# Attention into a mixture of experts on one core: later loads, split first weights, second weights behind the gathers

## The chip, the cores and the metric

The kernel runs on one core of a Trainium2 chip. The metric is the device time of one execution in microseconds. Three runs of the kernel before gave 662.02, 662.31 and 664.82 us, with a median of 662.31 us.

## The reference

Two blocks follow each other. The first is attention with 8 batches, 8 heads, 576 positions and a head size of 64. A position sees itself and the 127 before it, with a bias that falls linearly with distance by a slope of its own for each head. The second is a mixture of 8 experts over the 4608 rows of 512 that the attention gives: each row goes to the one expert with the largest gate logit.

```python
scores = scale * np.matmul(q, k.transpose(0, 1, 3, 2))
scores = np.where((rel >= 0) & (rel < 128), scores + bias[None], -1e9)
attn = softmax(scores)
x = np.matmul(attn, v)            # (8, 8, 576, 64) -> rows (4608, 512)
logits = x @ w_gate               # (4608, 8)
e = argmax(logits); g = softmax(logits)[e]
out[row] = g * (relu(x[row] @ w1[e]) @ w2[e])    # w1: 512 x 1024, w2: 1024 x 512
```

All of it is in float32.

## The kernel before

The order of the instructions on each engine is written out by hand: the program order is the order of issue, and semaphores hold an instruction until what it needs is there.

**The attention** is cut into 16 units. A unit (`units`) is a pair of batches `bp` (4 of them) and a pair of heads `hp` (4 of them), so four units make one batch pair. Each unit has four groups `g`, one for each two or three blocks of 64 keys, so there are 64 groups, and the loop `for i in range(NG)` goes over them. `scores(i)` (L785) computes the scores of group i on TensorE (L793), their exponentials on ScalarE (L802, L812) and a product with the distance factors on VectorE (L806); its result is the tile `prob[i]`. `scores_to` keeps the scores three or four groups ahead of the use. `values` (L823) multiplies the probabilities with the values (L836), `finish` (L844) copies the result to `xT`, `sums` (L861) makes the row sums (L875, L887).

**The loads** of queries, keys and values go through the queue of SyncE (SP). A unit has four parts: `load_part(u, g)` loads keys for g = 0, queries for g = 1 and half a tile of values for g = 2 and 3. Loads are paced: `no_earlier_than(there)` (L644) issues a tiny copy on SP that waits for a tile, so that what stands behind it on SP starts no earlier. In group i the pacing copy waits for `prob[i + 1]`, and part g of unit u + 2 follows. The first weights of expert 0 (`load_w1`, 2 MB) go out in groups 16 to 23 (units 4 and 5) in eight pieces of 256 KB.

**The routing** of a batch pair runs in the gaps of the next pair's attention: `behind(bp)` gives a list of small tasks, and `some()` takes one step of the list in each group. The steps are `gate` (gate logits on TensorE L895, added to the sums on VectorE L900), `turn` (L919), the scalings, `place` (the slot of each row, L1006), `ones_at` and `enlist` (the lists of rows by expert), and the rows themselves: `row_turned` transposes 128 rows on TensorE (L1106) and copies them on ScalarE (L1108), `row_out` adds their scales on GpSimd (L1115) and stores them to DRAM from GpSimd's queue (L1120). `row_tile` gives the tile for them. The first pair uses `squares_...` instead, which transposes on VectorE (L1157).

**The passage to the experts.** After the third pair's routing the rows of expert 0 are gathered: four indirect copies from GpSimd (L1346), each of 128 rows. When the loop over groups ends, the attention's pools are closed, the pools of the experts are opened in their place, the second weights of expert 0 (`load_w2`, 2048 KB, L570) are issued on SP, and then, in this order: the first tile's transposes (`to_columns`, L1379, into the banks `pair(2)`), the fourth pair's first gate, the second tile's transposes, the third tile's scaling (`to_scale`, L1365), and the other two gates. Each gate writes one of two PSUM buffers `m`, which its VectorE sum sets free.

**The experts.** `strassen1` and `strassen2` multiply with seven products in place of eight, over sums of weights and rows made on VectorE (`w1_sums` into `ws`, `x_sums` into `xs`, L541 to L544 into `w2s`). The first expert's `w1_sums` are eight tasks `ws_tasks`, taken in groups 33, 34, 35 and 45, 46, 47. The fourth pair's routing runs beside the first expert. The other experts and the left-over groups follow, with the next weights loaded behind each.

Of the kernel before, what the change touches and what calls it, by code (L numbers as in the profile page):

```python
# [8 lines left out]
F32 = mybir.dt.float32  # L9
# [7 lines left out]
P = 128  # L17
# [441 lines left out]
def kernel(  # L459
# [17 lines left out]
    F = moe_w1.shape[2]  # L477
# [6 lines left out]
    BP = N // S // 2  # L484
# [5 lines left out]
    NJ = 4  # L490
# [11 lines left out]
    NA = P // TQ  # L502
    PD = HP * TQ
    PW = PD + HP
    NR = 2

    x_d = nc.dram_tensor("x_rows", (N, NA * PW), F32, kind="Internal").ap()
    x_pieces = x_d.rearrange("n (a w) -> (n a) w", a=NA)

    with ExitStack() as fast:  # L510
# [5 lines left out]
        rte = pool(fast, "rte", 1)  # L516
        w1_a = pool(fast, "w1_a", 1)
        ws_pool = pool(fast, "weight_sums", 1)
        mx_pool = pool(fast, "moe_x", 1)
# [41 lines left out]
        def load_w1(g, w_pool, parts=slice(0, DB), cols=slice(0, F)):  # L561
            if "w1" not in g:
                g["w1"] = w_pool.tile([P, DB, F], F32, name="w1")
            nc.sync.dma_start(
                g["w1"][:, parts, cols], g["src"][0].rearrange("(a p) f -> p a f", p=P)[:, parts, cols],
            )

        def load_w2(g, w_pool):
            g["w2"] = w_pool.tile([P, FB, Dm], F32, name="w2")
            nc.sync.dma_start(g["w2"][:], g["src"][1].rearrange("(a p) d -> p a d", p=P))  # L570
# [18 lines left out]
        ps_s = pool(att, "ps_s", 2, space=PSUM)  # L589
# [5 lines left out]
        units = [(bp, hp) for bp in range(BP) for hp in range(HP)]  # L595
# [23 lines left out]
            )  # L619

        def load_part(u, g):
            if g == 0:
                load_k(u, 0, S, nc.sync)
            elif g == 1:
                load_q(u, 0, S, nc.sync)
            else:
                k0, k1 = ((0, 5), (5, NK))[u % 2]
                load_v(u // 2 * 2, g - 2, nc.sync, k0, k1)
# [9 lines left out]
        load_k(1, 0, S, nc.sync)  # L638
        load_q(1, 0, S, nc.sync)

        pace = rte.tile([1, 4 * len(units) + 1], F32, name="pace")
        paced = []

        def no_earlier_than(there):  # L644
            n = len(paced)
            paced.append(n)
            nc.sync.dma_start(pace[:, n : n + 1], there)
# [241 lines left out]
        def gate(bp, c):  # L889
            if bp not in gs:  # L890
                gs[bp] = xp.tile([P, 2 * S], F32, name="gs", bufs=1)
            ps = ps_m.tile([P, 512], F32, name="m")
            c0, n = ((0, LQ), (LQ, LQ), (2 * LQ, P))[c]
            for hp in range(HP):
                nc.tensor.matmul(  # L895
                    ps[32 * hp : 32 * hp + 32, :n], lhsT=wgd[:, hp, :], rhs=xT[bp][:, hp, c0 : c0 + n],
                    start=True, stop=True,
                )
            if c < 2:
                nc.vector.tensor_tensor(gs[bp][:, c0 : c0 + n], ps[:, :n], sumT[bp][:, :LQ], op=ALU.add)  # L900
            else:
                nc.vector.tensor_tensor(
                    gs[bp][:, c0 : c0 + n].rearrange("p (b q) -> p b q", b=2),
                    ps[:, :n].rearrange("p (b q) -> p b q", b=2),
                    sumT[bp][:, None, LQ:].to_broadcast([P, 2, S - LQ]), op=ALU.add,
                )
# [182 lines left out]
        last_rows = []  # L1089

        def row_tile(bp, t):
            if bp < 2 and t % 2:
                return more_rows[:, t // 2]
            if t in (1, 3, 5):
                if not last_rows:
                    x = mx_pool.tile([P, DB, NJ * P], F32, name="xgT").rearrange("p a b -> p (a b)")
                    last_rows.extend(
                        x[:, k * NA * PW : (k + 1) * NA * PW].rearrange("p (a w) -> p a w", a=NA) for k in range(3)
                    )
                return last_rows[t // 2]  # L1100
            return rows.tile([P, NA, PW], F32, name="xs")

        def row_turned(bp, t):
# [248 lines left out]
        def gather(g, src):  # L1352
            for f in gathers(g, src):
                f()
# [69 lines left out]
        def behind(bp):  # L1424

            g3 = [lambda k=k: gate(bp, k) for k in range(3)]
            t3 = [lambda k=k: turn(bp, k) for k in range(3)]
            rs = [lambda t=t: row(bp, t) for t in range(TPB)]
            a, a2, b, b2, c, n, q, p, p2, o, o2, e = (
                [lambda f=f: f(bp)] for f in (  # L1430
                    scale_a, scale_a2, scale_b, scale_b2, scale_c, count, scales_squared, place, place2, ones_at,
                    ones_at2, enlist,
                )
            )
            if bp == 0:
                rt = [lambda t=t: squares_turned(bp, t) for t in range(TPB)]
                ro = [
                    lambda t=t: (squares_scaled(bp, t), squares_out(bp, t, nc.gpsimd)) for t in range(TPB)
                ]
                return [g3[0:1], g3[1:2], g3[2:] + t3[0:1] + rt[0:1], t3[1:] + rt[1:3], a, a2, b, b2, c + n, rt[3:5],  # L1440
                        q + p, p2 + rt[5:6] + ro[0:2], o + ro[2:4], o2 + ro[4:5], rt[6:8] + ro[5:7],
                        e + rt[8:9] + ro[7:9]]
            rt, ro = ([lambda t=t, f=f: f(bp, t) for t in range(TPB)] for f in (row_turned, row_out))
            if bp == 1:
                return [g3[0:1], g3[1:2], g3[2:] + t3[0:1], t3[1:], a + rt[0:1], a2 + rt[1:2], b + rt[2:3],
                        b2 + rt[3:4], c + n, rt[4:5], p + ro[0:2], p2 + ro[2:5], o + rs[5:6], o2 + rs[6:7], rs[7:8],
                        e + rs[8:9]]
            return [g3, t3, a + a2, b + b2 + rt[0:1], c + n + rt[1:2], rt[2:4] + ro[0:2], p + p2 + ro[2:4] + rt[4:6],
                    o + o2 + ro[4:6] + rt[6:8], ro[6:8] + rs[8:9] + [early_holes], e + [early_table, lambda: gather(fixed[0], x_d[: 3 * 2 * S, :])]]

        tasks = []

        def some():
            if tasks:
                for f in tasks.pop(0):
                    f()

        NG = 4 * len(units)
        scored = [0]

        def scores_to(n):
            while scored[0] < min(n, NG):
                scores(scored[0])
                scored[0] += 1
# [7 lines left out]
        for i in range(NG):  # L1472
            u, g = divmod(i, 4)
            bp, hp = units[u]
            if u + 2 < len(units):
                no_earlier_than(prob[i + 1][0:1, 0, 0:1])
                load_part(u + 2, g)
            if u in (4, 5):
                d, c = u - 4 + g // 2 * 2, g % 2 * F // 2
                load_w1(fixed[0], w1_a, slice(d, d + 1), slice(c, c + F // 2))  # L1480
            if i == 1:
                token_numbers()
                table_consts()
            if i == 12:
                token_parts()

            ahead = i + (3 if u < 2 else 4)
            if g == 0:
                scores_to(ahead)
            if g == 0:  # L1490
                values(u, 0, (0, 1))
                if u < HP - 1:
                    factors(u + 1)
            elif g == 1:
                values(u, 0, (2, 3))
            elif g == 2:
                values(u, 0, (4,))
                finish(u, 0)
                sums(u)
                some()  # L1500
                scores_to(ahead)
                values(u, 1, (3, 4, 5))
            else:
                values(u, 1, (6, 7, 8))
                finish(u, 1)
            if u == len(units) - 1 and g == 1:
                first = [t for _, t in prepare(fixed[0])]
                tasks.extend([[], first[0] + first[1][1:]])
            if g != 2:
                some()  # L1510
            for _ in range({33: 1, 34: 1, 35: 2, 45: 1, 46: 1, 47: 2}.get(i, 0)):
                ws_tasks.pop(0)()
            if g in (1, 3):
                scores_to(ahead)
            if g == 3 and hp == HP - 1 and bp < BP - 1:
                tasks.extend(behind(bp))
        att.close()


# [29 lines left out]
        def pair(k):  # L1549

            i = (turn_of[0] + k) % 3
            return [mps.tile([P, 512], F32, name=f"pair{i}{c}") for c in "ab"]
# [277 lines left out]
            return [(g, t) for t in todo]  # L1830


        load_w2(fixed[0], w2_a)
        while tasks:
            some()
        g_of = [lambda k=k: gate(BP - 1, k) for k in range(3)]
        fixed[0]["banks"] = pair(2)
        for f in first[1][:1] + g_of[:1] + first[2] + g_of[1:]:
            f()
        for i in range(len(groups)):  # L1840
            g = groups[i]
            drain(g)
# [76 lines left out]
```

## Time and profile before

| what | value |
|---|---|
| median of three runs | 662.31 us (662.02 to 664.82) |
| the profiled execution's own time | 666.81 us |
| its span | 665.0 us |
| granted TensorE clock, mean | 0.993 |
| TensorE busy | 634.0 us, 95% |
| VectorE busy | 366.7 us, 55% |
| ScalarE busy | 215.5 us, 32% |
| GpSimd busy | 271.6 us, 41% |
| queue q1 (loads from SP) | 92.51 MB, 43.8% of the DMA engines' span |
| queue q0 (GpSimd's copies) | 27.38 MB, 13.0% |

The profile is of one execution. Its span runs from the first to the last instruction, and its own time is that of the whole execution. A row of the timeline begins with start and duration in us, then engine, line, operation, the tile written and the tiles read, with shapes. A count stands for several merged instructions, and what ended the idle time before the row stands in brackets. "SPq" and "POOLq" are the queues of SyncE and GpSimd, where an issue of a copy is seen, not its transfer. "issue" is idle time for which the profile shows no releaser.

### The profile page before, as it was taken

The page shows a single profiled execution, that of the slowest core. Times are in us where ns is not written, and L with a number is a line of the kernel's source. Part 1 is how long each engine was busy: PE and PEld are TensorE (multiplying, and loading weights), DVE is VectorE, ACT ScalarE, POOL GpSimd, SP SyncE. Part 2 cuts the span into 40 slices and gives each one's busy share as a digit, 9 for nine tenths or more (in the row PEclk, how much of TensorE's full clock was granted, in tenths as well). Part 3 has the DMA queues.
Part 4 walks back from the last instruction along what each step waited for, and adds up shares of the span by engine and source line. Part 5 has one row for each costly group of instructions (what it writes and reads, how often), then busy time and mean ns, then how long its engine had stood idle before and what let it go on. Part 6 is the DMA issues. An engine that isn't in the chain of part 4 may idle for free.

```text
span 665.0 us, 14491 instructions
## 1 busy us (share of the span) xinstructions
PE 634.0 (95%) x5824; PEld 529.9 (80%) x5824; DVE 366.7 (55%) x745; ACT 215.5 (32%) x493; POOL 271.6 (41%) x459
## 2 busy tenths in 40 slices
PE   6899799899899999999999999999999999999993
PEld 5778678678797888978888887888788978887883
DVE  3457858777598768435743662385148425643410
ACT  6767467576330231023102301221131023102310
POOL 8100772225032585466167515642563366130002
PEclk9999999999999999999999999999999999999998
DMA  9889987855438944591377319542934581366002
GB/s 262 242 252 249 269 230 230 270 183 153 153 84 259 356 126 155 187 307 37 137 242 262 124 52 321 173 151 81 313 128 144 170 314 41 133 227 238 0 1 73
DMA packets 55503, 121.80 MB, mean 183 GB/s; under 512 B 5841, under 2 KB 21361, under 8 KB 55426
## 3 DMA queue, kind: packets, MB, share of 16 engines
q1 hardware_dynamic: 43650, 92.51, 43.8%
q0 software_dynamic: 10624, 27.38, 13.0%
q8 instruction: 48, 0.79, 0.5%
q10 hardware_dynamic: 1152, 0.88, 0.4%
q14 instruction: 29, 0.24, 0.1%
HBM read 101.58 MB, written 19.63 MB: 182 GB/s over the span
## 4 chain that ended last, share of the span: by engine, by line
PE 68%; issue 10%; DVE 7%; DMA 2%; POOL 2%; ACT 0%; POOLq 0%; DVEq 0%
PE pair0a L1669 4%; PE pair1b L1669 4%; PE pair1a L1669 4%; PE pair0b L1669 4%; PE pair1a L1602 4%; PE sp L793 4%; PE pair1b L1602 4%; PE pair0b L1602 4%; PE pair2a L1669 4%; PE pair2b L1669 4%; PE pair2b L1602 3%; PE at L836 3%; PE pair2a L1602 3%; PE pair0a L1602 3%; PE pair0a L1727 2%
## 5 line engine op out<-in xcount | busy, mean ns | idle before, releaser
L1346 POOL DMA_INDIRECT xg<-x_rows,p_idx x121 | 128.4, 1061 | 33.7 <-issue 28.0
L1694 POOL DMA_INDIRECT out_dram<-zo,s_idx x38 | 43.4, 1142 | 173.2 <-DVE zo L1683 144.7
L806 DVE TENSOR_TENSOR pe<-pe,fac 128x512 f32<-128x512 f32 x64 | 43.9, 690 | 42.2 <-ACT pe L802 42.2
L793 PE MATMUL sp<-q_sb,k_sb 64*64 64x192 f32 (+2 forms) x1152 | 57.8, 325 | 7.6 <-DMA q_sb<-in_qT_dram 5.2
L836 PE MATMUL at<-pe,v_sb 64*64 64x192 f32 (+2 forms) x1408 | 57.1, 284 | 5.2 <-issue 4.5
L836 PEld LDWEIGHTS at<-pe,v_sb 64*64 64x64 f32 x1408 | 48.7, 135 | 11.8 <-issue 6.3
L793 PEld LDWEIGHTS sp<-q_sb,k_sb 64*64 64x64 f32 x1152 | 42.2, 139 | 16.6 <-issue 6.6
L802 ACT ACTIVATE pe<-sp 128x512 f32<-128x512 f32 x64 | 38.4, 600 | 30.5 <-issue 13.7
L812 ACT ACTIVATE pe<-sp,mid 128x128 f32<-128x128 f32 x128 | 40.1, 372 | 0.0
L1616 ACT ACTIVATE h<-h 128x512 f32<-128x512 f32 (+1 forms) x32 | 20.0, 624 | 39.0 <-DVE h L1615 39.0
L1365 DVE TENSOR_TENSOR xn<-xg 128x512 f32<-128x512 f32 (+1 forms) x39 | 25.8, 663 | 5.9 <-DMA xg<-x_rows,g_idx 4.6
L875 PE MATMUL m<-pe,ind 128*32 128x192 f32 (+2 forms) x576 | 26.2, 311 | 1.0 <-DVE pe L806 0.7
L1544 POOL COPY paced_by<-h 1x1 f32<-1x1 f32 x47 | 18.5, 394 | 19.7 <-DVE h L1718 15.8
L875 PEld LDWEIGHTS m<-pe,ind 128*32 128x32 f32 x576 | 19.3, 109 | 6.4 <-ACT pe L812 1.4
L1383 DVE STREAM_TRANSPOSE xgT<-xn 128x512 f32<-128x512 f32 (+1 forms) x31 | 21.6, 698 | 1.1
L541 DVE TENSOR_TENSOR w2s<-w 128x512 f32<-128x512 f32 x16 | 10.9, 684 | 19.6 <-DMA w<-in_moe_w_dram 19.6
L855 ACT COPY xT<-at 128x640 f32<-128x640 f32 (+1 forms) x32 | 18.9, 591 | 8.4 <-PE at L836 8.3
L1165 POOL COPY xs<-sq 128x16 f32<-128x16 f32 x6 | 1.2, 207 | 49.6 <-ACT sq L1143 49.6
L1176 POOL DMA_DIRECT2D x_rows<-xs x32 | 17.3, 553 | 5.6 <-DVE h L1615 2.3
L1669 PE MATMUL pair1a<-w,h 128*128 128x256 f32 x72 | 17.1, 380 | 0.0
L1669 PE MATMUL pair1b<-w,h 128*128 128x256 f32 (+1 forms) x72 | 17.0, 379 | 0.0
L1602 PE MATMUL pair0a<-xgT,w 128*128 128x256 f32 (+1 forms) x72 | 16.7, 375 | 0.0
(417 smaller groups left out, 1398.3 us busy)
## 6 DMA issues: line engine op xcount, KB each, us to landing
w<-in_moe_w_dram SPq DMA_DIRECT2D x29, 2048.0 KB
k_sb<-in_kT_dram SPq DMA_DIRECT2D x15, 576.0 KB
q_sb<-in_qT_dram SPq DMA_DIRECT2D x15, 576.0 KB
v_sb<-in_v_dram SPq DMA_DIRECT2D x14, 320.0 KB
v_sb<-in_v_dram SPq DMA_DIRECT2D x14, 256.0 KB
x_rows<-xs POOLq DMA_DIRECT2D x9, 264.0 KB, 3.8
x_rows<-xT SPq DMA_DIRECT2D x8, 264.0 KB
w<-in_moe_w_dram SPq DMA_DIRECT2D x8, 256.0 KB
```

The lines of the kernel that those rows point to most:

```text
L793: nc.tensor.matmul(by_distance(sp[c * KB : (c + 1) * KB, r, :GC], kb, 0, n), lhsT=k_sb[u][hs, c, kb * KB : (kb + 1) * KB], rhs=q_sb[u][hs, ...
L802: nc.scalar.activation(outer, sp[:, :, :GC].rearrange("p r (j x) -> p r j x", j=3)[:, :, 0:3:2, :], AF.Exp, scale=SCALE,)
L806: nc.vector.tensor_tensor(outer, outer, fac[:, h0 : h0 + 2, : 2 * w].rearrange("p r (j x) -> p r j x", j=2)[:, :, :, : 2 * KB], op=ALU.mult,)
L812: nc.scalar.activation(pe[:, r, inner], sp[:, r, inner], AF.Exp, bias=mid[:, h0 + r : h0 + r + 1], scale=SCALE,)
L836: nc.tensor.matmul(acc[r * D : (r + 1) * D, c, lo - q0 : hi - q0].rearrange("p (j x) -> p j x", x=KB), lhsT=v_sb[u // 2][c * KB : (c + 1) ...
L875: nc.tensor.matmul(sm[32 * j : 32 * j + 32, lo - q0 : hi - q0].rearrange("p (j x) -> p j x", x=KB), lhsT=ind[:, hp, :], rhs=by_distance(pe ...
L1346: nc.gpsimd.indirect_dma_start(out=to, out_offset=None, in_=where, in_offset=bass.IndirectOffsetOnAxis(ap=idx, axis=0),)
L1365: nc.vector.tensor_tensor(xn[:, :m], x, s.unsqueeze(3).to_broadcast([P, m, HP, TQ]), op=ALU.mult)
L1383: nc.vector.transpose(to[:, :, : m * TQ].rearrange("p h (k j) -> p k h j", j=TQ), xn[:, :m])
L1602: nc.tensor.matmul(ps[:, f * n : (f + 1) * n], lhsT=left[m][:, d, fb * P : (fb + 1) * P], rhs=right[m][:, d, :], start=(m in (1, 2, 5) and ...
L1669: nc.tensor.matmul(ps, lhsT=left[m][:, f, c * P : c * P + q], rhs=right[m][:, f, :], start=(m in (1, 2, 5) and f == 0), stop=True, skip_gr ...
L1694: ins = nc.gpsimd.indirect_dma_start(out=out[:, :], out_offset=bass.IndirectOffsetOnAxis(ap=s_idx[:n, g["c0"] + j : g["c0"] + j + 1], axis=0),
```

## The change

Five things are edited.

1. **Loads.** The loop issues part m of the loads behind `prob[m - 5]` where it was `prob[m - 7]`, after the scores of that group are issued. The guard in `load_part` covers the last groups, for which only the pacing copy is left.
2. **First weights of expert 0.** They go out in 16 pieces of 128 KB, eight in groups 16 to 23 (rows 0 and 2 of the four blocks of rows) and eight in groups 46 to 53 (rows 1 and 3). The second four of `ws_tasks` move from groups 45 to 47 to groups 58, 59, 62 and 63.
3. **Second weights of expert 0.** Their load moves behind a pacing copy that waits for the last gathered tile of expert 0.
4. **Pools.** The first transposes, the gates and the third tile's scaling are issued before the attention's pools are closed. Their banks come from the scores' pool, not from `pair(2)`.
5. **Row work.** In the third pair five row tiles, not three, come from buffers of the experts; the steps are regrouped, and row tile 8 leaves before tile 7. In the first pair `place` moves into the next step.

```diff
@@ load_part
+            if u >= len(units):
+                return
@@ row_tile
-            if t in (1, 3, 5):
+            if bp == 2 and t in (1, 3, 5, 7, 8):
                 if not last_rows:
                     x = mx_pool.tile([P, DB, NJ * P], F32, name="xgT").rearrange("p a b -> p (a b)")
+                    y = mx_pool.tile([P, 3, 2, 256], F32, name="xs").rearrange("p a b c -> p (a b c)")
                     last_rows.extend(
-                        x[:, k * NA * PW : (k + 1) * NA * PW].rearrange("p (a w) -> p a w", a=NA) for k in range(3)
+                        m[:, k * NA * PW : (k + 1) * NA * PW].rearrange("p (a w) -> p a w", a=NA)
+                        for m, n in ((x, 3), (y, 2)) for k in range(n)
                     )
-                return last_rows[t // 2]
+                return last_rows[t // 2 if t < 8 else 4]
@@ behind, bp == 0
-                        q + p, p2 + rt[5:6] + ro[0:2], o + ro[2:4], o2 + ro[4:5], rt[6:8] + ro[5:7],
+                        q, p + p2 + rt[5:6] + ro[0:2], o + ro[2:4], o2 + ro[4:5], rt[6:8] + ro[5:7],
@@ behind, bp == 2
-            return [g3, t3, a + a2, b + b2 + rt[0:1], c + n + rt[1:2], rt[2:4] + ro[0:2], p + p2 + ro[2:4] + rt[4:6],
-                    o + o2 + ro[4:6] + rt[6:8], ro[6:8] + rs[8:9] + [early_holes], e + [early_table, lambda: gather(fixed[0], x_d[: 3 * 2 * S, :])]]
+            return [g3, t3, a + a2, b + b2 + rt[0:1], c + n + rt[1:2], rt[2:5] + ro[0:2], p + p2 + ro[2:5],
+                    rt[5:7] + rt[8:9] + o + o2 + ro[5:7], rt[7:8] + ro[8:9] + ro[7:8] + [early_holes], e + [early_table, lambda: gather(fixed[0], x_d[: 3 * 2 * S, :])]]
@@ the loop over groups
-            if u + 2 < len(units):
-                no_earlier_than(prob[i + 1][0:1, 0, 0:1])
-                load_part(u + 2, g)
-            if u in (4, 5):
-                d, c = u - 4 + g // 2 * 2, g % 2 * F // 2
-                load_w1(fixed[0], w1_a, slice(d, d + 1), slice(c, c + F // 2))
+            if u in (4, 5) or 46 <= i < 54:
+                n = i - 16 if i < 24 else i - 46
+                d, c = n % 2 * 2 + (i >= 24), n // 2 * 256
+                load_w1(fixed[0], w1_a, slice(d, d + 1), slice(c, c + 256))
...
-            for _ in range({33: 1, 34: 1, 35: 2, 45: 1, 46: 1, 47: 2}.get(i, 0)):
+            for _ in range({33: 1, 34: 1, 35: 2, 58: 1, 59: 1, 62: 1, 63: 1}.get(i, 0)):
                 ws_tasks.pop(0)()
             if g in (1, 3):
                 scores_to(ahead)
+            while loaded[0] < scored[0]:
+                no_earlier_than(prob[loaded[0]][0:1, 0, 0:1])
+                load_part(*divmod(loaded[0] + 5, 4))
+                loaded[0] += 1
...
+        both = ps_s.tile([P, 2, 512], F32, name="sp")
+        fixed[0]["banks"] = [both[:, 0, :], both[:, 1, :]]
+        while tasks:
+            some()
+        g_of = [lambda k=k: gate(BP - 1, k) for k in range(3)]
+        for f in first[1][:1] + g_of[:1] + first[2] + g_of[1:]:
+            f()
         att.close()
@@ the experts
+        no_earlier_than(fixed[0]["xg"][0:1, NJ - 1, 0, 0:1])
         load_w2(fixed[0], w2_a)
-        while tasks:
-            some()
-        g_of = [lambda k=k: gate(BP - 1, k) for k in range(3)]
-        fixed[0]["banks"] = pair(2)
-        for f in first[1][:1] + g_of[:1] + first[2] + g_of[1:]:
-            f()
```

More of the change, by code (lines that the diff above doesn't have):

```diff
@@ L639 @@
         load_q(1, 0, S, nc.sync)
-        pace = rte.tile([1, 4 * len(units) + 1], F32, name="pace")
+        pace = rte.tile([1, 4 * len(units) + 2], F32, name="pace")
         paced = []
@@ L1458 @@
         NG = 4 * len(units)
-        scored = [0]
+        scored, loaded = [0], [3]
         def scores_to(n):
```

## The prediction

> **What bounds the kernel now.** I read the page first, then the busy time by stage, then who TensorE waits for from the second stage on. The page gives the span; the stages are the attention (0 to 165 us), the passage from it into the experts (165 to 176), the first expert with the last routing beside it (176 to 210), and the other experts.
>
> ```profile
> span 665.0 us, 14491 instructions
> ...
> 60.00:90.00 30.00, 25.66 (x551) 20.22 (x547) 23.68 (x58) 15.43 (x45) 17.92 (x37) 0.94 0.95 257
> ...
> 110.00:130.00 20.00, 17.88 (x389) 14.07 (x381) 15.01 (x33) 12.97 (x34) 8.82 (x20) 1.00 0.85 289
> 130.00:165.00 35.00, 33.98 (x776) 28.25 (x767) 25.31 (x74) 24.23 (x61) 11.81 (x22) 1.00 0.56 172
> 165.00:176.00 11.00, 8.53 (x72) 5.55 (x64) 4.12 (x7) 3.82 (x9) 1.26 (x1) 1.00 0.74 255
> 176.00:210.00 34.00, 32.70 (x176) 29.79 (x177) 32.55 (x83) 9.87 (x23) 5.64 (x17) 1.00 0.40 101
> 210.00:640.00 430.00, 429.22 (x2112) 360.86 (x2111) 220.70 (x387) 89.19 (x171) 197.81 (x242) 1.00 0.52 176
> ```
>
> Columns after the stretch: its length, busy time of TensorE, its weight loads, VectorE, ScalarE and GpSimd, then granted clock, DMA share and GB/s. From 210 on TensorE is busy 429.2 of 430 us: nothing the change touches there can shorten it, but what is won before 176 is carried to the end whole, if no wait eats it. The waits after 176 are few; these are all but one of 0.2:
>
> ```profile
> PE m L1072 <- DVE gsr L1062: 0.7, 1, 0.7
> PE pair2a L1602 <- DVE xs L542: 0.5, 1, 0.5
> PE pair2b L1602 <- DVE h L1626: 0.5, 1, 0.5
> ```
>
> So the change is decided in the attention and at the passage. Between 176 and 210 VectorE is busy 32.55 of 34 us, so it must start earlier too for a gain to survive.
>
> **The second weights behind the gathers.** These are the rows of the passage, TensorE, VectorE, GpSimd and the load queue (SPq) from the timeline, and the landing times of the four gathers:
>
> ```profile
> 165.96 0.66 PE L1379 MATMUL pair2a<-ident,xn 128*128 128x128 f32 x4 [0.80 <-ACT xT L857]
> 169.34 1.78 PE L1602 MATMUL pair0a<-xgT,w 128*128 128x224 f32 x8
> 172.74 0.66 PE L1379 MATMUL m<-ident,xn 128*128 128x128 f32 x4 [1.62 <-DVE gs L900]
> ...
> 166.00 0.69 DVE L1365 TENSOR_TENSOR xn<-xg 128x512 f32<-128x512 f32 x1 [0.45 <-DMA xg<-x_rows,g_idx]
> 167.74 0.69 DVE L900 TENSOR_TENSOR gs<-m,sumT 128x512 f32<-128x512 f32 x1 [1.04 <-PE m L895]
> 171.40 0.69 DVE L1365 TENSOR_TENSOR xn<-xg 128x512 f32<-128x512 f32 x1 [2.97 <-DMA xg<-x_rows,g_idx]
> 174.05 0.69 DVE L1365 TENSOR_TENSOR xn<-xg 128x512 f32<-128x512 f32 x1 [1.16 <-DMA xg<-x_rows,g_idx]
> 188.16 0.64 DVE L541 TENSOR_TENSOR w2s<-w 128x512 f32<-128x512 f32 x1
> ...
> 163.85 0.95 POOL L1346 DMA_INDIRECT xg<-x_rows,g_idx  x1 [0.30 <-issue]
> 165.11 1.26 POOL L1346 DMA_INDIRECT xg<-x_rows,g_idx  x1 [0.30 <-issue]
> ...
> 163.85 0.39 SPq L570 DMA_DIRECT2D w<-in_moe_w_dram  x1
> ...
> DMA to landing us min/median/max: 3.7/7.4/8.8
> ```
>
> The 2048 KB load starts at 163.85, in the same instant as the third gather. The quickest gather landed after 3.7 us, the slowest after 8.8. VectorE stands at the third tile's scaling (L1365) until 171.40, and behind it in its queue stand the two gate sums (L900) that free a PSUM buffer; TensorE waits for the first of them, 1.62 us until 172.74. With the load behind the last gather, the third lands at about 163.85 + 3.7 = 167.6 and the fourth at 168.8. VectorE then runs: gate sum at about 168.0 (it also has two moved weight sums of 0.69 in front of it), scaling 168.7, gate sum 169.4 to 170.1. TensorE: first transposes at 165.6 instead of 165.96, since the new buffer hangs on old scores and not on the copy at L857; gates and second transposes as now; the last gate waits for the gate sum until 168.8; first product 169.1 to 170.8; third transposes at 170.8 instead of 172.74. **Term: -1.9 us.** Bounds: -3.0, if the whole wait of 2.97 comes off; 0, if the gathers are slow for another reason. I take the worked chain. VectorE's sums start as much earlier, since they follow the fourth tile, whose wait goes too.
>
> What is late instead is the load itself: issued at about 168.8 + 0.6 for the pacing copy instead of 163.85, thus 5.5 us later. It landed by about 175 while it shared the queues, so now by 180 or 181; its first reader is at 188.16, or 186.3 when moved up. Hidden, with 5 us over. The pacing copy waits on SP with the weights and, much later, the row stores of the last batches behind it; none is due before 190.
>
> **Loads two groups later.** A load of part m was paced by group m-7 and is now by m-5. A query tile (q_sb) is the tightest: its lead falls from six groups to four, some 10 of 15 us at 165 us / 64 groups. Unit 7 has the least room. Its load went out at 56.56; the new pace is the one that now stands at 60.11, and its first scores stand at 63.66:
>
> ```profile
> 56.56 0.38 SPq L602 DMA_DIRECT2D q_sb<-in_qT_dram  x1
> ...
> 60.11 0.59 SPq L647 DMA_DIRECT2D pace<-pe  x1
> ...
> 146.10 0.68 SPq L616 DMA_DIRECT2D v_sb<-in_v_dram  x1
> ...
> 63.66 0.65 PE L793 MATMUL sp<-q_sb,k_sb 64*64 64x192 f32 x10
> ...
> 67.50 0.65 DVE L806 TENSOR_TENSOR pe<-pe,fac 128x512 f32<-128x512 f32 x1
> ...
> q1 hardware_dynamic: 49, 0.04, 12.7%
> ```
>
> The last row is the load queue's traffic between 150 and 151 us, its last before the expert weights: the load issued at 146.10 was through 4 to 5 us later. So unit 7 lands at 60.7 + 4 to 5 = 64.7 to 65.7 and TensorE could stand 1.0 to 2.0 us. But VectorE finishes that group's probabilities only at 68.15, 4.5 us behind its scores, because its queue is full there; TensorE meets other waits right after (below), which such a delay would absorb. **Term: +0.5**, bounds 0 and +2.0. The other units have 0 to 8 us to spare by the same reckoning; I take nothing for them here.
>
> **First weights in halves.** Half of them leaves the eight groups of units 4 and 5, from 43.63 on, and goes to groups 46 to 53, whose first pacing copy stands at 117.60, so to about 117 to 142 us; the pieces are 128 KB now. Units 4 and 5 show no loss to win back. In the new place the DMA share is 0.85 (110 to 130). TensorE's idle times there, and the dearest ones earlier, have no releaser in the trace ("issue") and stand in the middle of a run of like matmuls:
>
> ```profile
> 43.63 0.44 SPq L564 DMA_DIRECT2D w<-in_moe_w_dram  x1
> ...
> 117.60 0.58 SPq L647 DMA_DIRECT2D pace<-pe  x1
> ...
> 73.79 0.34 PE L793 MATMUL sp<-q_sb,k_sb 64*64 64x64 f32 x6 [1.13 <-issue]
> 80.72 1.42 PE L836 MATMUL at<-pe,v_sb 64*64 64x128 f32 x36 [2.04 <-issue]
> 82.86 2.84 PE L793 MATMUL sp<-q_sb,k_sb 64*64 64x192 f32 x40
> ...
> 118.50 0.45 PE L836 MATMUL at<-pe,v_sb 64*64 64x128 f32 x7 [0.97 <-issue]
> 125.45 0.55 PE L836 MATMUL at<-pe,v_sb 64*64 64x128 f32 x12 [0.95 <-issue]
> 126.88 1.54 PE L793 MATMUL sp<-q_sb,k_sb 64*64 64x192 f32 x40
> ...
> 83.00:84.00 1.00, 1.00 (x16) 0.78 (x20) 0.89 (x2) 0.00 (x0) 0.89 (x3) 0.50 0.98 169
> ```
>
> They come only where the DMA queues are full (shares 0.95 and 0.85 in the stage rows). I read them as TensorE's own instructions arriving late by DMA; the trace only suggests that. More traffic at 117 to 142 can double the two there: +1.9 at most, 0 at least. **Term: +0.3**, nearer to none since 130 to 165 has a share of 0.56.
>
> The weight sums (L533 to L536) of the second half, four of about 0.68 us on VectorE, move from about 120 to 128 us to about 159 to 168. Two fit into the idle time before the probabilities at 161; two stand before the gate sum, reckoned above. **Term: 0**; without that cover 1.4 us.
>
> **The reordered row work.** In the first batch the placing moves one step back, in the third every tile of rows has its own buffer, and the eighth leaves before the seventh.
>
> ```profile
> 68.85 0.39 PE L1006 MATMUL m<-pre,lt_strict 128*128 128x8 f32 x2 [0.65 <-ACT sq L1143]
> 146.86 1.07 PE L1106 MATMUL m<-ident,xT 128*128 128x128 f32 x8 [0.76 <-DVE sumT L887]
> 147.57 0.59 ACT L1108 COPY xs<-m 128x512 f32<-128x512 f32 x1 [1.75 <-POOL xgT L1115]
> ```
>
> The wait at L1006 (0.65) ends with a copy that the placing would no longer follow at once: -0.3, bounds 0 and -0.65. ScalarE's wait for a free row tile (1.75) goes; TensorE's beside it (0.76) has a VectorE releaser and may stay: -0.4, bounds 0 and -0.76. The last store leaves perhaps half a us sooner; the first tile's scaling is held by VectorE, so this is 0. The six more pacing copies on SP (0.59 each) fall while SP waits anyway: 0. Pools closed later move no work: 0.
>
> **Sum:** -1.9 + 0.5 + 0.3 + 0 - 0.3 - 0.4 = -1.8 us. The profiled execution took 666.81 us by its own time, 1.8 around its span of 665.0, and so would take 665.0. It lies 4.5 above the median of the runs shown, 662.31; I carry the difference over to them: **660.5 us**.
>
> **Rivals.** *The stalls go.* With less traffic at 43 to 63 and the loads re-timed, the two stalls at 72.66 and 78.68 vanish: 1.13 + 2.04, and the half clock after the second (the 40 score matmuls took 2.84 instead of 1.54, clock 0.50), 1.30: together 4.5 us, hence 660.5 - 4.5 = 656.0. For it: they sit just behind the first weights' loads. Against it: the volume between 70 and 80 us stays the same, and the row stores too.
>
> The Trainium skill, TensorE: Matmul & The Clock Gate, section "Part 1: The HAM clock gate (the "warmup" mystery)", has the array fall to half clock after about 3.4 us of idling. By that rule a stall of 2.04 us would cost no clock, and this rival would end at 657.3. Here the clock row shows 0.50 some 3 us after such a stall, so the measurement decides.
>
> *The passage wins nothing.* The gathers are slow by their own scattered reads, or VectorE's unbroken queue until 210 keeps the end where it was: 660.5 + 1.9 = 662.4. For it: VectorE's 32.55 of 34 us. Against it: the first gather's 3.7 us, and VectorE's own waits of 2.97 and 1.16 on gathers.
>
> *The later loads starve the scores: slower.* Place: the scores (L793) at q_sb. Landing needs 4 to 5 us and the room is 1 to 4 us in most of units 2 to 8 and 11. The point from which it decides: a landing 2 us longer than now. Then unit 7 stands for 3 to 4 us, and some five others for 0.5 each: about +6 in place of +0.5, thus 666.0, and more if a stall halves the clock. For it: DMA share 0.95 at 60 to 90. Against it: the loads are spread over the groups and no more than two are under way.
>
> **How the numbers follow.** Forecast 0.50, stalls gone 0.21, nothing won 0.17, slower 0.12. The forecast's own range is 658.5 to 662 from its terms' bounds. A measurement of this kernel tells about 0.5%, 3.3 us, from no change: faster means below 659.0, slower above 665.6. Faster: 0.21 and the low tail of the forecast, 0.09, make 0.30. Slower: 0.12. Same: 0.58. For 8 in 10 I go from 655.5 to 664.5, which leaves out the slower case and the far half of the first rival.
>
> **What would show it.** The 2048 KB load issued after the last gather's landing, near 169; landing of all four gathers below 5 us; the wait of 1.62 at the third transposes gone, the first product of the first expert as early as 169; its weights before 186. At unit 7 a wait of TensorE on q_sb of a us or so. Stalls named "issue" near 72, 78, 118 and 125 still there in sum. The prediction is wrong if the score matmuls wait on q_sb or k_sb in several units, if those stalls go away together, or if the stage after 176 grows by what the passage saved.

## The result and the profile after

The changed kernel is **slower**: 671.97 us (median of six runs, 669.55 to 676.2) against 663.91 us for the kernel before (662.02 to 668.44, six runs beside them). The ratio is 1.0111 with a 95% interval of 1.0074 to 1.0149. The profiled execution took 675.13 us by its own time, with a span of 673.3.

The stages of the kernel after, in the columns of the prediction's first view:

```profile
60.00:90.00 30.00, 24.87 (x594) 19.98 (x595) 25.27 (x61) 16.10 (x46) 14.72 (x30) 1.00 0.84 243
110.00:130.00 20.00, 15.27 (x333) 12.68 (x329) 11.32 (x27) 10.55 (x27) 7.72 (x17) 0.96 0.93 297
...
165.00:176.00 11.00, 9.00 (x141) 6.26 (x137) 3.68 (x7) 2.90 (x7) 3.75 (x4) 0.70 0.45 107
176.00:210.00 34.00, 33.46 (x207) 29.85 (x200) 28.53 (x73) 12.69 (x28) 5.62 (x17) 1.00 0.40 116
210.00:640.00 430.00, 428.48 (x2092) 360.44 (x2092) 228.33 (x402) 88.61 (x170) 197.67 (x242) 1.00 0.53 180
```

From 176 on TensorE is as full as before, so the loss lies ahead of that. Between 110 and 130 TensorE works 15.27 of 20 us, where it worked 17.88; between 165 and 176 its clock is 0.70. Whom it waits for up to 175 us (total, times, longest), and the rows of those waits with the issue of the query loads they belong to:

```profile
PE sp L795 <- DMA q_sb<-in_qT_dram: 13.4, 6, 4.3
```

```profile
33.35 0.38 SPq L602 DMA_DIRECT2D q_sb<-in_qT_dram  x1
...
62.49 0.37 SPq L602 DMA_DIRECT2D q_sb<-in_qT_dram  x1
...
82.99 0.38 SPq L602 DMA_DIRECT2D q_sb<-in_qT_dram  x1
...
111.28 0.38 SPq L602 DMA_DIRECT2D q_sb<-in_qT_dram  x1
```

```profile
39.09 0.88 PE L795 MATMUL sp<-q_sb,k_sb 64*64 64x192 f32 x16 [1.64 <-DMA q_sb<-in_qT_dram]
68.56 0.88 PE L795 MATMUL sp<-q_sb,k_sb 64*64 64x192 f32 x16 [3.21 <-DMA q_sb<-in_qT_dram]
88.90 0.88 PE L795 MATMUL sp<-q_sb,k_sb 64*64 64x192 f32 x16 [1.45 <-DMA q_sb<-in_qT_dram]
119.22 0.88 PE L795 MATMUL sp<-q_sb,k_sb 64*64 64x192 f32 x16 [1.98 <-DMA q_sb<-in_qT_dram]
```

Pair each issue with the scores that waited for it. The time between them is 5.7, 6.1, 5.9 and 7.9 us (units 4, 7, 9 and 12). These are the scores starving in several units, the slower rival.

The passage, from the end of the last value matmuls to the third transposes, reads as forecast, only later:

```profile
173.49 2.80 PE L838 MATMUL at<-pe,v_sb 64*64 64x64 f32 x48
...
181.29 0.60 PE L1383 MATMUL m<-ident,xn 128*128 128x128 f32 x4
...
178.65 0.68 DVE L1369 TENSOR_TENSOR xn<-xg 128x512 f32<-128x512 f32 x1
...
173.79 0.40 SPq L570 DMA_DIRECT2D w<-in_moe_w_dram  x1
```

The waits of 1.62 (TensorE on a gate sum) and 2.97 us (VectorE on the third gather) are gone. The passage is 5.0 us (173.49 + 2.80 to 181.29). In the profile before it was 7.58 (163.61 + 1.55 = 165.16, to 172.74):

```profile
162.15 1.54 PE L875 MATMUL m<-pe,ind 128*32 128x192 f32 x36
163.61 1.55 PE L836 MATMUL at<-pe,v_sb 64*64 64x64 f32 x48
```

In front of it stands something that was not foreseen. TensorE works off its matmuls there in bursts of about five every 0.7 us, with no releaser, and then at half clock: the 36 row sums behind it took 2.79 us, and 1.54 in the profile before (first row above).

```profile
166.84 0.55 PE L838 MATMUL at<-pe,v_sb 64*64 64x192 f32 x5 [0.19 <-issue]
...
170.47 0.38 PE L838 MATMUL at<-pe,v_sb 64*64 64x64 f32 x2 [1.08 <-issue]
170.78 2.79 PE L877 MATMUL m<-pe,ind 128*32 128x192 f32 x36
```

So there were two suspects: the query loads, and this slow stretch beside the gathers.

### The profile page after: what moved, and what is told of

Read it like the earlier page. It is cut to its first block, busy times and chain, and to the rows that moved or that the text cites. A ratio compares the mean times of both kernels' runs of the same rounds, so it can differ in the third digit from the quotient of the medians.

```text
span 673.3 us, 14511 instructions
## 1 busy us (share of the span) xinstructions
PE 637.9 (95%) x5824; PEld 532.3 (79%) x5824; DVE 366.6 (54%) x745; ACT 215.0 (32%) x493; POOL 271.1 (40%) x459
## 4 chain that ended last, share of the span: by engine, by line
PE 68%; issue 10%; DVE 8%; DMA 6%; POOL 1%; ACT 1%; SPq 0%; POOLq 0%; DVEq 0%; ACTq 0%
PE pair0a L1682 4%; PE pair1b L1682 4%; PE pair1a L1682 4%; PE pair0b L1682 4%; PE pair1a L1615 4%; DMA q_sb<-in_qT_dram 4%; PE at L838 4%; PE pair1b L1615 4%; PE pair0b L1615 4%; PE pair2a L1682 4%; PE pair2b L1682 4%; PE pair0a L1615 4%; PE sp L795 4%; PE pair2b L1615 3%; PE pair2a L1615 3%
## 5 line engine op out<-in xcount | busy, mean ns | idle before, releaser
L838 PE MATMUL at<-pe,v_sb 64*64 64x192 f32 (+2 forms) x1408 | 59.5, 292 | 6.0 <-issue 4.7
L857 ACT COPY xT<-at 128x640 f32<-128x640 f32 (+1 forms) x32 | 18.9, 590 | 13.0 <-PE at L838 12.8
```

Source lines behind the costliest of these rows:

```text
L838: nc.tensor.matmul(acc[r * D : (r + 1) * D, c, lo - q0 : hi - q0].rearrange("p (j x) -> p j x", x=KB), lhsT=v_sb[u // 2][c * KB : (c + 1) ...
```

## The experiments

The kernels ran in three sets, each beside shared runs of the kernel before. Those had medians of 665.03, 661.89 and 662.28 us in the three sets, so ratios are compared first, and times only within a set.

### First set: which part costs

**`undo_loads`**: the changed kernel, loads as before.

```diff
         for i in range(NG):
+            if u + 2 < len(units):
+                no_earlier_than(prob[i + 1][0:1, 0, 0:1])
+                load_part(u + 2, g)
...
-            while loaded[0] < scored[0]:
-                no_earlier_than(prob[loaded[0]][0:1, 0, 0:1])
-                load_part(*divmod(loaded[0] + 5, 4))
-                loaded[0] += 1
```

> The changed kernel with the loads paced two groups earlier again, as before the change; everything else stays changed. Theory lateness (the scores stand at late query tiles: 13.4 us of waits on q_sb against 5.2 before): the waits fall back to about 5, the attention ends some 8 us earlier than in the changed kernel, and with the 2.6 us won at the passage the kernel is 2 to 3 us faster than before the change, ratio about 0.996. Theory instruction supply (the stalls named issue and the half clock near 127 and 166 to 176 us come from the moved first weights): the kernel stays slower than before by 3 to 6 us, ratio 1.005 to 1.01, with those stalls still there.

Measured: 662.85 us, ratio 0.998 (0.9956 to 1.0004). The loss is gone, as lateness has it; that this kernel is faster than the one before, as it also has it, this set does not show.

**`loads_alone`**: the kernel before with nothing but the later loads (the reverse of that diff).

> The kernel before with the loads two groups later and nothing else changed. Theory lateness: waits on q_sb of 10 us or more and 6 to 10 us slower than before, ratio 1.010 to 1.015. Theory instruction supply: at most 3 us slower, ratio under 1.005, the waits on q_sb being eaten by other waits.

Measured: 674.91 us, ratio **1.0145** (1.0102 to 1.0187). That is 9.9 us. The one edit that the prediction priced at +0.5 us makes the whole loss.

**`undo_w1`**: the changed kernel with the first weights as before.

```diff
-            if u in (4, 5) or 46 <= i < 54:
-                n = i - 16 if i < 24 else i - 46
-                d, c = n % 2 * 2 + (i >= 24), n // 2 * 256
-                load_w1(fixed[0], w1_a, slice(d, d + 1), slice(c, c + 256))
+            if u in (4, 5):
+                d, c = u - 4 + g // 2 * 2, g % 2 * F // 2
+                load_w1(fixed[0], w1_a, slice(d, d + 1), slice(c, c + F // 2))
...
-            for _ in range({33: 1, 34: 1, 35: 2, 58: 1, 59: 1, 62: 1, 63: 1}.get(i, 0)):
+            for _ in range({33: 1, 34: 1, 35: 2, 45: 1, 46: 1, 47: 2}.get(i, 0)):
```

> The changed kernel with the first weights of expert 0 and their sums as before the change; loads stay two groups later. Theory lateness: still 6 to 10 us slower than before, ratio about 1.011, as the changed kernel, and with the full first weights between 43 and 63 us the query wait at unit 7 grows above 3.2 us. Theory instruction supply: the stall of 2.75 us near 127 is back to about 1 and the half clock after it is gone, so 4 us or more are won against the changed kernel, ratio about 1.005.

Measured: 674.62 us, ratio 1.0147 (1.0107 to 1.0187). The dearest stall without a releaser, 2.75 us at 127.00 in the kernel after, stands as well without the halves:

```profile
128.08 0.55 PE L838 MATMUL at<-pe,v_sb 64*64 64x128 f32 x12 [2.48 <-issue]
```

So the moved weight traffic does not make it, and that theory falls. The wait of unit 7 is 3.31 us here and 3.21 with the halves, so they hardly bear on it either.

**`passage_alone`**: the kernel before with the gates ahead of the closing of the pools, and the pacing copy ahead of the second weights.

```diff
+        both = ps_s.tile([P, 2, 512], F32, name="sp")
+        fixed[0]["banks"] = [both[:, 0, :], both[:, 1, :]]
+        while tasks:
+            some()
+        g_of = [lambda k=k: gate(BP - 1, k) for k in range(3)]
+        for f in first[1][:1] + g_of[:1] + first[2] + g_of[1:]:
+            f()
         att.close()
...
+        no_earlier_than(fixed[0]["xg"][0:1, NJ - 1, 0, 0:1])
         load_w2(fixed[0], w2_a)
-        while tasks:
-            some()
-        g_of = [lambda k=k: gate(BP - 1, k) for k in range(3)]
-        fixed[0]["banks"] = pair(2)
-        for f in first[1][:1] + g_of[:1] + first[2] + g_of[1:]:
-            f()
```

> The kernel before with only the second weights behind the gathers and the pools closed behind the gates. Lateness and instruction supply both expect the 2.6 us that the changed kernel's trace shows from the last value matmul to the third transposes: 2 to 3 us faster, ratio 0.996. A third theory, that the earlier and quicker gathers starve TensorE's own instructions at the end of the attention (166 to 171 us in the changed kernel): a slow stretch and half clock before the first transposes here too, and 1 us or more slower than before.

Measured: 664.85 us, ratio 0.9994 (0.9968 to 1.002): no gain that can be told. All four profiles of this set have the slow stretch beside the gathers, the two without the later loads as well, so it does not come from the loads.

The waits on q_sb follow the loads. These are the rows for `undo_loads`, `loads_alone` and `undo_w1`, in this order:

```profile
PE sp L793 <- DMA q_sb<-in_qT_dram: 6.3, 2, 4.3
```

```profile
PE sp L795 <- DMA q_sb<-in_qT_dram: 12.4, 7, 4.4
```

```profile
PE sp L795 <- DMA q_sb<-in_qT_dram: 12.8, 6, 4.2
```

The first holds only the two waits at the very start, before any paced load.

### Second set: how much room, for which tile, and the passage

**`one_later`**: the changed kernel, loads by m-6, one group later than before.

```diff
-        scored, loaded = [0], [3]
+        scored, loaded = [0], [2]
-                load_part(*divmod(loaded[0] + 5, 4))
+                load_part(*divmod(loaded[0] + 6, 4))
```

> The changed kernel with its loads one group later than before instead of two (a part of number m is paced by group m-6). Lateness theory (the scores stand for query tiles that land 5.7 to 7.8 us after their issue): each query load goes out one group, about 2.6 us, earlier than in the changed kernel, so of the four waits of 1.64, 3.21, 1.45 and 1.98 us only unit 7's keeps some 0.6; waits on q_sb 6.3 to 8 us, ratio 0.998 to 1.002. Rival (each group of delay costs the same, through where the loads fall among the row stores): half of the loss between the kernel with the loads as before (0.998) and the changed one (1.011) stays, ratio about 1.005.

Measured: 659.71 us, ratio 0.998 (0.9948 to 1.0012). The waits on q_sb are 5.9 us, of which 5.1 are those of the start; the rest is one wait of 0.81 us, at unit 8 and not at unit 7. With the loads as before the ratio is 0.998 and, later, 0.9944, and with two groups it is 1.0111 and 1.0128. So the first group costs 0 to 0.4% and the second 1.3 to 1.5%: a threshold, as lateness has it, and not so much per group.

**`queries_early`**: the changed kernel with the queries alone back at m-7.

```diff
-                no_earlier_than(prob[loaded[0]][0:1, 0, 0:1])
-                load_part(*divmod(loaded[0] + 5, 4))
+                if loaded[0] % 4:
+                    no_earlier_than(prob[loaded[0]][0:1, 0, 0:1])
+                if loaded[0] % 4 and loaded[0] > 2:
+                    load_part(*divmod(loaded[0] + 5, 4))
+                if loaded[0] % 4 == 2:
+                    load_part(*divmod(loaded[0] + 7, 4))
```

> The changed kernel with the query loads alone back at group m-7; keys and values stay at m-5. Lateness theory: the only tile with too little room was the query tile, so waits on q_sb fall to those of the start, 6.3 us, none appears on k_sb or v_sb beyond 0.5 us, ratio 0.997 to 1.000. Rival (two groups less of everything crowd the queues, or the keys are next in line, their lead being one group more than the queries' had): waits of 1 us and more on k_sb or v_sb, or stalls without a releaser, and a ratio of 1.005 or more.

Measured: 664.36 us, ratio 1.0054 (1.0026 to 1.0081). The rival was right in its number, and the keys are next in line:

```profile
PE sp L795 <- DMA q_sb<-in_qT_dram: 4.8, 2, 4.2
PE sp L795 <- DMA k_sb<-in_kT_dram: 4.6, 3, 2.7
...
PE at L838 <- DMA v_sb<-in_v_dram: 1.1, 1, 1.1
```

The keys are paced by m-5 in both kernels, and the kernel after has no wait on them. I read this as lateness that shows only where TensorE does not stand for the queries first; that the earlier queries crowd the keys' loads is not ruled out. Either way, moving one tile back uncovers the next.

**`w2_with_gathers`**: the changed kernel with the loads as before and without the pacing copy.

```diff
-        no_earlier_than(fixed[0]["xg"][0:1, NJ - 1, 0, 0:1])
         load_w2(fixed[0], w2_a)
```

> The changed kernel with the loads as before, and without the pacing copy that holds the second weights behind the fourth gather; the gates and the closing of the pools stay as in the changed kernel. Theory (the 2048 KB load slows the gathers): VectorE again stands about 3 us at the third tile's scaling, end of values to third transposes goes from 5.4 to 7 to 7.6 us, time about 2 us more than with the pacing copy, ratio about 1.001. Rival (the passage was won by the order of the gates and the buffers): passage stays at 5 to 5.5 us, ratio 0.998.

Measured: 656.42 us, ratio **0.9934** (0.9899 to 0.9969), faster than the kernel before. The price in my theory failed: VectorE does not stand for 3 us at the third tile, and the passage is 5.42 us (156.60 to 162.02) without any pacing copy. The last gather, the load, the last value matmuls and the third transposes:

```profile
154.24 0.95 POOL L1348 DMA_INDIRECT xg<-x_rows,g_idx  x1 [0.30 <-issue]
...
155.28 0.40 SPq L570 DMA_DIRECT2D w<-in_moe_w_dram  x1
...
155.05 1.55 PE L836 MATMUL at<-pe,v_sb 64*64 64x64 f32 x48
...
162.02 0.60 PE L1381 MATMUL m<-ident,xn 128*128 128x128 f32 x4
```

The load goes out at 155.28 by itself just when the last gather has been issued (154.24 + 0.95). With the load beside them, the slowest gather lands later. These are the landing times of the four gathers here and in `undo_loads_again` (third set), which has the pacing copy:

```profile
DMA to landing us min/median/max: 3.4/4.0/7.4
DMA to landing us min/median/max: 3.6/4.0/4.9
```

But TensorE does not wait for it at the third transposes.

**`before_again`**: the kernel before, unchanged, for a second profile.

> The kernel before, unchanged, for a second profile of it. Theory (TensorE is slowed by the gathers whatever the loads): a stretch of some 4 us from 1.3 to 1.8 us after the first gather to 1 us after the last one's issue, in which TensorE works in bursts of about five matmuls every 0.7 us. Rival (the stretch belongs to the changed parts): none, as in the first profile of it, 7.6 us from the end of the values to the third transposes. The stalls without a releaser near 73 and 79 us are expected somewhere else or of another length, if they come from instruction supply that is not tied to one place.

Measured: one execution, 659.15 us. It has no slow stretch, and its stalls without a releaser stand at 29.30 (1.09 us), 35.18 (0.82), 73.19 (0.58) and 79.57 (1.49). The same rows of the passage:

```profile
158.34 0.94 POOL L1346 DMA_INDIRECT xg<-x_rows,g_idx  x1 [0.30 <-issue]
...
157.76 0.39 SPq L570 DMA_DIRECT2D w<-in_moe_w_dram  x1
...
157.51 1.55 PE L836 MATMUL at<-pe,v_sb 64*64 64x64 f32 x48
...
164.83 0.60 PE L1379 MATMUL m<-ident,xn 128*128 128x128 f32 x4
...
166.53 0.69 DVE L1365 TENSOR_TENSOR xn<-xg 128x512 f32<-128x512 f32 x1 [1.88 <-DMA xg<-x_rows,g_idx]
```

Here the load is issued ahead of the last gather, and VectorE waits 1.88 us for the fourth tile. Yet the passage is only 5.77 us (159.06 to 164.83), and 5.78 in `loads_alone`, which has the same passage (172.29 + 2.53 to 180.60). The 7.58 on which the prediction's largest gain was built came from one execution.

### Third set: the loss again, and what the rest is worth

**`after_again`**: the changed kernel.

> The changed kernel as it is, timed beside the three below. Theory (the later query loads cost the time, the slow stretch beside the gathers only blurs it): q_sb waits of 10 us or more in all, with unit 7's above 2 us, and a ratio of 1.008 to 1.014 whether the slow stretch shows or not. Rival (the slow stretch and its half clock made half of the loss): without the stretch in the profile the ratio falls to 1.005 or less.

Measured: 671.54 us, ratio 1.0128 (1.0055 to 1.02). Its profile has **no** slow stretch, and the loss is there all the same: the stretch is not its cause. TensorE also works slower behind the waits. This is unit 7's wait, with a stretch of 1 us behind it (granted clock third from the right):

```profile
67.59 1.56 PE L795 MATMUL sp<-q_sb,k_sb 64*64 64x192 f32 x16 [3.58 <-DMA pace<-pe]
...
68.00:69.00 1.00, 1.00 (x20) 0.86 (x16) 0.00 (x0) 0.00 (x0) 0.00 (x0) 0.50 1.02 222
```

The releaser is given as the pacing copy here; that it is the query load of unit 7 (issued at 60.92) is read from its place, where the kernel after waits 3.21 us on q_sb.

**`undo_loads_again`**: the kernel `undo_loads`, a second time.

> The changed kernel with the loads as before, and with the pacing copy that holds the second weights behind the fourth gather, beside the same kernel without that copy. Theory (the copy is not needed, since the buffer of the second weights comes free only when the gathers are out, and it costs nothing either): ratio 0.992 to 0.995, the same as without it within 0.3%. Rival (the copy costs time: the second weights start 6 to 8 us later and the first expert or the sums wait for them): ratio 0.997 to 0.999, and waits on the second weights or their sums between 176 and 210 us.

Measured: 657.96 us, ratio 0.9944 (0.991 to 0.9977). Against `after_again` in the same set, the later loads cost 13.6 us.

This kernel differs from `after_again` in the loads alone, and neither profile has the slow stretch, so the two can be laid side by side. TensorE's waits on loads and its busy time up to the same point, here (3388 matmuls):

```profile
PE sp L793 <- DMA q_sb<-in_qT_dram: 5.0, 2, 4.3
...
0.00:163.50 163.50, 150.31 (x3388) 120.86 (x3389) 109.72 (x270) 112.19 (x291) 62.17 (x195) 1.00 0.85 241
```

and in `after_again` (3388):

```profile
PE sp L795 <- DMA q_sb<-in_qT_dram: 11.1, 6, 4.2
PE sp L795 <- DMA pace<-pe: 3.6, 1, 3.6
...
0.00:175.00 175.00, 153.28 (x3388) 122.95 (x3389) 110.01 (x270) 112.49 (x291) 62.84 (x195) 0.97 0.76 225
```

The same work takes 11.5 us longer. Of that 3.0 are matmuls that ran slower (153.28 - 150.31) and 8.5 are idle (21.72 - 13.19). On loads alone TensorE waits 9.7 us more (11.1 + 3.6 - 5.0). The other waits together are shorter by 1.2. The first scores of unit 7 and the last values, here:

```profile
63.97 0.83 PE L793 MATMUL sp<-q_sb,k_sb 64*64 64x192 f32 x16
...
157.80 1.55 PE L836 MATMUL at<-pe,v_sb 64*64 64x64 f32 x48
```

and the last values in `after_again`:

```profile
169.16 1.55 PE L838 MATMUL at<-pe,v_sb 64*64 64x64 f32 x48
```

Unit 7 is 3.6 us later there (67.59 against 63.97), unit 9 is 6.9 (90.24 against 83.30), and the last values are 11.4. Next to nothing of what is lost is made up.

The rival, that the pacing copy costs time, has no sign of it in the profile: TensorE waits for no second weights between 176 and 210 us.

**`w2_again`**: the kernel `w2_with_gathers`, a second time.

> The changed kernel with the loads as before and without the pacing copy, a second time. If it beats the kernel before in earnest: ratio 0.990 to 0.996 again. If the first measurement was luck: 0.997 or more.

Measured: 657.37 us, ratio **0.9917** (0.9885 to 0.9948). It beats the kernel before in both sets, and the changed one by 14 us. Its interval overlaps that of `undo_loads_again`: the pacing copy is neither needed nor shown to cost.

**`gates_rows`**: `w2_with_gathers` with the first weights as before (the diff of `undo_w1`).

> The same without the first weights in halves: only the gates and pools and the reordered row work are changed against the kernel before. Theory (the halves are worth 1 to 2 us, by the fewer stalls without a releaser in units 7 to 8): ratio 0.2 to 0.3% above the kernel with them, about 0.996, and stalls without a releaser of 2 to 4 us in the profile. Rival (the gain is in the gates and rows): ratio the same within 0.1%.

Measured: 658.42 us, ratio 0.9944 (0.9915 to 0.9974). The halves are worth about 1 us or nothing; this is undecided. So the gain of this kernel lies in the gates, the pools and the row work; which of them makes it, no run tells apart.

## Why the prediction was wrong

**The failing step is "Loads two groups later": "Term: +0.5, bounds 0 and +2.0".** It was 9.9 us by `loads_alone` and 13.6 by the third set. Four things in it were wrong.

- **The landing.** It was priced at 4 to 5 us, from when the queue's traffic ended after a values load, at a quiet time. Queries are 576 KB by the page and values 256 or 320. From issue to scores it took 5.7 to 7.9 us in the kernel after, and 4.5 to 7.4 in `after_again` (unit 3, 25.43 to 29.95; unit 12, 114.00 to 121.41). With 6.1, unit 7 reckons out as 60.7 + 6.1 - 63.66 = 3.1 us, and 3.21 was measured: there the room was right, and the landing was mis-sized.
- **"The other units have 0 to 8 us to spare; I take nothing for them here."** A unit with nothing to spare pays the whole error of the landing, as unit 4 did (1.64 us). For units 9 and 12 the room was wrong too. By the profile before it is 9.2 and 7.9 us: their scores stand at 88.97 and 119.47, and the new pacing copies at 79.13 and 110.93, with 0.6 for the copy. In the kernel after it was 4.5 and 6.0 (88.90 - 1.45 - 82.99 and 119.22 - 1.98 - 111.28). Part of the room was stalls of that one execution: the one of 2.04 us with its half clock lies in unit 9's, the one of 0.97 in unit 12's.
- **The clock.** Nothing was taken for it. In `after_again` it is about 3.0 of the 11.5 us.
- **The overlap.** The other waits, which were to absorb unit 7's, did not. They gave back 1.2 us in all, against 9.7 more on loads.

**The slower rival** had the place and the mechanism right. Its point of decision, "a landing 2 us longer", is about what was met, since 5.7 to 7.9 stand against 4 to 5. Its price of +6 was too low against 9.9 to 13.6: it put some five other units at 0.5 us each, where three paid 1.45 to 1.98 in the kernel after, and left the half clock to an "and more". It got a chance of only 0.12. What spoke against it, that the loads are spread and few are under way, was no argument about the time of one load.

**The range.** "658.5 to 662 from its terms' bounds" does not come out of the bounds. Added up they give -4.4 and +3.9 us, so 657.9 to 666.2. The measured time lies above that too, since the bound of +2.0 for the loads was itself too low.

**Second weights behind the gathers, -1.9.** Between the first profiles of the two kernels it was 2.6 us (7.58 and 5.0). The reason given, that the 2048 KB load slows the gathers, holds: the slowest landing was 3.9 and 4.9 us with the load held back (`after_again`, `undo_loads_again`), and 6.3 to 8.8 in the five profiles that have the load beside the gathers and show the landings. What failed is the step from there to TensorE. A late gather held up the third transposes in one execution only; by chance it was the one that the prediction read. Otherwise the passage is 5.77 and 5.78 us without this edit and 5.40 to 5.46 with the gates moved, whether the pacing copy is there or not (5.0 in the kernel after). So 0.35 us are won, and not by the pacing copy. They fit a step that the prediction had inside this term, the first transposes that no longer wait for the copy at L857 (165.6 instead of 165.96). That the load can come late without harm was right: in the kernel after TensorE waits for no weights between 175 and 215 us.

**Row work, -0.3 and -0.4.** Right in kind and about right in size. Both waits, at `place` and at the rows' transposes, still stand in `loads_alone`, which hasn't these edits:

```profile
PE m L1108 <- DVE sumT L889: 0.8, 1, 0.8
...
PE m L1008 <- ACT sq L1145: 0.6, 1, 0.6
```

In the kernel after neither is among the waits, which is 1.4 us. But three new ones stand there, as in every kernel with the new row work:

```profile
PE m L1074 <- DVE hole L1245: 0.4, 1, 0.4
PE m L1110 <- ACT xs L1112: 0.3, 1, 0.3
...
PE m L1110 <- ACT xgT L1112: 0.2, 1, 0.2
```

That leaves 0.5 us.

**First weights, +0.3, and the weight sums, 0.** No loss was found; the first can't be told from zero.

**The stalls go.** They did in the kernel after at 72.66 and 78.68, but they also shrink in `before_again`, the same kernel as before (0.58 and 1.49 instead of 1.13 and 2.04). Their lengths vary from execution to execution, and a price read from one profile doesn't belong to a change.

Without the loads the other edits gave -4.3 us (`undo_loads_again`, 662.28 to 657.96). In the first set it was -2.2, with an interval that includes no change. The prediction had -2.3 for them, inside both intervals, but not for its reasons: -1.9 of it was the second weights. The waits that the profiles tie to these edits make about 0.9 us (0.35 at the passage, 0.5 in the row work). Where the rest comes from stays open.

## What to carry to other kernels

When a load is moved later, take the time from issue to first use from that load's own rows, of its size and in its busiest stage, not from another transfer at a quiet time; then go through every consumer, since one with no room pays in full. Add the half clock that can follow a wait of TensorE. And before a gain is built on one wait, or a room on one profile, see whether a second profile of the same kernel has that wait and that room.

## What the runs showed of the hardware

- **Waits of TensorE and the clock.** In `after_again` waits of 3.58, 2.19 and 1.93 us were followed by granted clocks of 0.50. In `one_later` a stall of 2.23 us was followed by full clock:

```profile
35.69 0.76 PE L838 MATMUL at<-pe,v_sb 64*64 64x192 f32 x15 [2.23 <-issue]
...
36.00:37.00 1.00, 1.00 (x41) 1.00 (x35) 0.00 (x0) 0.37 (x1) 0.00 (x0) 1.00 0.60 186
```

  So the length of the wait alone doesn't decide. The Trainium skill, TensorE: Matmul & The Clock Gate, section "Part 1: The HAM clock gate (the "warmup" mystery)", says that activity is judged over a free-running window of about 3.4 us and that an idle window halves the clock. That the same wait can be dear or free fits a window which runs by itself; that 1.93 us were enough doesn't fit a window that must be idle throughout. The traces show how much idling was enough. In each profile the half clock begins and ends on one grid of 3.41 us. With the attention cut along that grid, this is the stretch with the stall of 2.23 us in `one_later`, and the one with the stall of 1.93 in `after_again`, which was followed by half clock:

```profile
33.92:37.33 3.41, 1.64 (x49) 1.64 (x52) 0.18 (x1) 0.65 (x2) 0.00 (x0) 1.00 0.69 186
...
125.58:128.99 3.41, 1.48 (x36) 1.14 (x28) 0.69 (x1) 0.92 (x4) 1.14 (x2) 1.00 0.99 371
```

  TensorE was busy 48% of the first and 43% of the second. In the 14 profiles, from 13 us on, all 13 such stretches with less than 47% were followed by half clock, and two of the ten between 48 and 55%. So here a wait was dear when it took more than about half of one stretch.
- **A slow stretch beside the gathers.** It stands in the profile after and in all four of the first set, whatever was edited, and in none of the eight later profiles, nor in the first of the kernel before. It starts one to two us after the first gather is issued and lasts about 4 us. Where it met the end of the attention, half clock followed (0.70 between 165 and 176). No edit brings it or takes it away, so it isn't part of this change's effect; its cause stays open.
- **Stalls without a releaser** in runs of like matmuls come in nearly every profile, 0.2 to 2.75 us long, and their lengths differ between two executions of the same kernel. Their places do not. The stalls at 127.00 in the kernel after, 122.51 in `one_later`, 128.37 in `after_again` and 125.45 in the kernel before all stand behind the same 2493 matmuls and 2493 weight loads. Up to 160 us, the places at which any of the 14 profiles stalls for over 0.5 us are 252 to 254 such instructions apart, or a multiple of that. This fits TensorE's own instructions arriving late, in blocks; no run here tests that.
